# Windowed attention and routed experts on one core: interleaving the two, with block-diagonal attention and a different softmax denominator

## The chip, the cores and the metric

The kernel runs on one core of one Trainium2 chip. The metric is the device time of that core for one whole execution, in microseconds (us). Runs of one kernel are quoted as a median. Each run also has a granted TensorE clock, averaged over its span as a share of full speed. One execution of each kernel was taken with a profile. Profile times are from the start of that execution's span.

In the profile's lines PE is TensorE's matmuls, PEld its weight loads, DVE is VectorE, ACT is ScalarE, POOL is GpSimd. `L128` is line 128 of that kernel's source. Line numbers differ between kernels, so follow the tile names.

## The reference

Sliding-window causal attention over 8 batches, 8 heads, 576 positions and head size 64 (window 64), followed by a mixture of 8 experts with one expert per batch. The expert is chosen from the mean over the positions of that batch's attention output.

```python
scores = scale * np.matmul(q, k.transpose(0, 1, 3, 2))
mask = (rel >= 0) & (rel < 64)                 # rel = query position - key position
attn = softmax(np.where(mask, scores, -1e9))
x = matmul(attn, v) -> [B, 576, 512]

pooled = x.mean(axis=1)                        # [B, 512]
e_idx  = argmax(pooled @ w_gate, axis=1)       # one expert for a whole batch
gate_w = softmax(logits)[e_idx]
out[b] = gate_w[b] * (relu(x[b] @ w1[e]) @ w2[e])   # 512 -> 1024 -> 512
```

One fact of this decides what can overlap: batch b's expert is not known until all of batch b's attention is done, but it does not depend on any other batch.

## The kernel before

The kernel has two stages. The first walks over 32 head pairs (8 batches, 4 pairs). Two heads sit in the two halves of the partitions, so most matmuls are pairs of 64x64 ones:

```python
for bb in range(B):
    for hp in range(NHP):
        # ... loads: q, k, v of both heads, runs of 256 B in HBM ...
        vt = asb.tile(...);  nc.scalar.copy(out=vt, in_=vn)          # cast of v
        for (tl, dst) in ((qn, qT), (kn, kT)):                       # transposes
            for st in range(4):
                nc.tensor.matmul(out=tp[:, ts(st, 128)], lhsT=tl[:, st]..., rhs=ident, ...)
            nc.scalar.copy(out=dst[:, 0:512], in_=tp)
            # ... the last 64 columns in the same way ...
        stage_a2(preva)      # scores of the pair before
        stage_b(prevb)       # values and denominator of the pair before that

def stage_a2(st):
    # 18 matmuls 64x64: sps / tp4 <- kT, qT
    nc.scalar.activation(out=pt[:, 0:8, :], in_=sps, func=AF.Exp, scale=scale)
    nc.scalar.activation(out=pt[:, 8, :], in_=tp4, func=AF.Exp, scale=scale)
    nc.vector.tensor_tensor(out=pt, in0=pt, in1=bandm, op=ALU.mult)  # the band mask

def stage_b(prev):
    # 40 matmuls 64x64: avp <- pt, vt (values);  lbp <- pt, ones64 (denominator)
    nc.scalar.copy(out=avs, in_=avp[:, 0:S])
    nc.scalar.copy(out=lbs, in_=lbp[:, 0:S])
    nc.vector.reciprocal(out=rl, in_=lbs)
    nc.vector.tensor_tensor_reduce(out=xT[:, pbb, php, :], in0=avs, in1=rl, ...
                                   accum_out=pooled[:, php, pbb:pbb + 1])
```

The second stage computes the gates of all 8 batches at once, and then one expert after another:

```python
# ... gates: 4 small matmuls, max, max_index, Exp, reciprocal ...
for bb in range(B):
    # ... loads of w1t and w2t of the chosen expert, cast on the way, 1 MB each in fp16 ...
    for ft in range(8):                            # w1: 64 matmuls, 288 columns each
        # ... php <- w1t, xT ...
        nc.scalar.activation(out=hT[:, ft]..., in_=php[:, :, 0:SC], func=AF.Relu, scale=gwb[:, bb:bb + 1])
    for mt in range(NST):                          # w2: 40 matmuls, 512 columns each
        # ... pso <- hT, w2t ...
        nc.vector.tensor_copy(out=ob[0:n], in_=pso[0:n])
        nc.sync.dma_start(out=out[bb, mt * 128:mt * 128 + n, :], in_=ob[0:n])
```

The softmax here doesn't subtract the row's maximum and nothing guards it: scores larger than these inputs give would overflow.

## Time and profile before

| before | value |
|---|---|
| median of the first 4 runs | 359.99 us (359.88 to 360.04) |
| mean granted clock of the profiled run | 0.776 |
| attention, 9 to 206.7 us | 197.7 us |
| gate and first weights, 206.7 to 217.6 us | 10.9 us |
| experts, 217.6 to 353.6 us | 136.0 us |

The page of the kernel before: the busy time of each engine, then its busy tenths in 40 slices of the span (9 means 90% or more), the granted clock in the same slices, and the DMA packets.

```profile
...
PE 283.4 (79%) x3018; PEld 196.3 (55%) x3018; DVE 190.1 (53%) x179; ACT 185.5 (52%) x356; POOL 130.8 (37%) x189
...
PE   0697878787778786877784216999999999999995
...
DVE  0049997888887978888879920122120303030312
...
PEclk9998565655655656556558556999999999999999
...
DMA packets 141234, 46.91 MB, mean 131 GB/s; under 512 B 124304, under 2 KB 132496, under 8 KB 141200
...
```

PE is 79% busy over the whole span, but its row and the clock row show two different halves. Up to about slice 21 PE is mostly at 7 to 8 tenths and, after a fast start, its clock at 5 to 6; in the last 15 slices both are at 9, but for the end. Busy at a lower clock is not the same work: the first 64 matmuls of w1 took 9.71 us at a mean clock of 0.82, later ones 8.04 us at 1.0. DVE is at 8 tenths in the first half and nearly free in the second.

The same by stage. After the stretch and its length, the columns are: busy us (and instructions) of PE, PEld, DVE, ACT and POOL, the mean granted clock, the DMA share, GB/s.

```profile
...
9.00:206.70 197.70, 146.62 (x2182) 114.31 (x2182) 161.27 (x130) 135.16 (x287) 109.47 (x156) 0.63 1.05 98
206.70:217.60 10.90, 0.80 (x4) 0.60 (x4) 0.97 (x7) 0.56 (x3) 3.28 (x4) 0.50 0.62 104
217.60:353.60 136.00, 135.96 (x832) 81.38 (x832) 26.91 (x39) 47.38 (x64) 9.82 (x12) 0.99 0.94 183
...
```

The middle line is a hole: 0.80 us of PE in 10.9 us. In the third line PE has no gap left: 135.96 us in 136.00. In the first line no engine is full: DVE, the fullest, has 161.27 of 197.70 us, 82%. (The DMA share adds up packets that overlap in time, so 1.05 there does not mean a full DMA.)

Two groups of the kernel before: line, engine, operation, tiles and shapes, count, then busy us and mean ns, then the idle time of the engine just before them.

```profile
...
L128 DVE RECIPROCAL rl<-lbs 128x576 f32<-128x576 f32 x32 | 119.9, 3750 | 25.8 <-ACT lbs L127 25.8
...
L261 DVE COPY ob<-pso 128x512 f32<-128x512 f32 (+1 forms) x40 | 27.6, 690 | 117.2 <-PE pso L257 102.6
...
```

The reciprocal takes 3750 ns for 576 elements per partition, so 119.9 us of the 161 that DVE is busy in attention. A plain copy of 512 elements out of PSUM takes 690 ns.

Its chain of waits, followed back from the last instruction, as shares of the span by engine and by line:

```profile
...
PE 70%; ACT 15%; issue 5%; DVE 4%; DMA 4%; POOL 1%; POOLq 0%; ACTq 0%; DVEq 0%
PE pso L257 20%; PE php L245 18%; PE tp L171 9%; PE lbp L116 8%; ACT pt L101 7%; PE sps L94 6%; PE avp L116 6%; ACT qT L175 5%; DMA w1t<-in_moe_w_dram 2%; DVE rl L128 2%; PE tp L176 2%; ACT kT L175 2%; DMA qn<-in_q_dram 1%; ACT qT L180 1%; 
...
```

### The profile page before, as it was taken

Reading aid. Unit: us, or ns where it says so; the run is one execution under the profiler, and the core shown is the slowest. Engines: PE = TensorE matmul, PEld = TensorE weight load, DVE = VectorE, ACT = ScalarE, POOL = GpSimd, SP = SyncE. Lnnn points to the kernel's source line nnn. Section 1 sums busy time; section 2 is a strip of 40 time slices with the busy share of each in tenths; the row PEclk is TensorE's granted clock in tenths of the full one; section 3 lists DMA queues with packets and bytes.
Section 4 is the critical chain, followed back from the end, with each engine's and each line's share of the span. In section 5 each row is a group of like instructions: output and inputs, shape, how many; then the busy total and the mean of one; then the engine's idle time right before and its main releaser. Section 6 shows DMA issues by size and latency. Waiting matters only on the chain.

```text
span 357.8 us, 7472 instructions
## 1 busy us (share of the span) xinstructions
PE 283.4 (79%) x3018; PEld 196.3 (55%) x3018; DVE 190.1 (53%) x179; ACT 185.5 (52%) x356; POOL 130.8 (37%) x189
## 2 busy tenths in 40 slices
PE   0697878787778786877784216999999999999995
PEld 0475656565656565656563204565647474756562
DVE  0049997888887978888879920122120303030312
ACT  2578777777766767777766102332415160605140
POOL 9969656565656566666500030000000011100000
PEclk9998565655655656556558556999999999999999
DMA  9999999999999999999800049999999999999302
GB/s 125 173 160 142 127 119 94 113 99 116 99 115 94 115 99 114 100 111 100 78 3 2 0 65 198 209 264 180 211 174 222 178 230 179 203 212 156 132 29 105
DMA packets 141234, 46.91 MB, mean 131 GB/s; under 512 B 124304, under 2 KB 132496, under 8 KB 141200
## 3 DMA queue, kind: packets, MB, share of 16 engines
q0 software_dynamic: 96416, 27.26, 77.1%
q1 hardware_dynamic: 44784, 19.18, 21.0%
q8 instruction: 24, 0.39, 0.5%
q14 instruction: 10, 0.08, 0.1%
HBM read 63.95 MB, written 9.44 MB: 205 GB/s over the span
## 4 chain that ended last, share of the span: by engine, by line
PE 70%; ACT 15%; issue 5%; DVE 4%; DMA 4%; POOL 1%; POOLq 0%; ACTq 0%; DVEq 0%
PE pso L257 20%; PE php L245 18%; PE tp L171 9%; PE lbp L116 8%; ACT pt L101 7%; PE sps L94 6%; PE avp L116 6%; ACT qT L175 5%; DMA w1t<-in_moe_w_dram 2%; DVE rl L128 2%; PE tp L176 2%; ACT kT L175 2%; DMA qn<-in_q_dram 1%; ACT qT L180 1%; DVE xT L129 1%
## 5 line engine op out<-in xcount | busy, mean ns | idle before, releaser
L128 DVE RECIPROCAL rl<-lbs 128x576 f32<-128x576 f32 x32 | 119.9, 3750 | 25.8 <-ACT lbs L127 25.8
L249 ACT ACTIVATE hT<-php,gwb 128x576 f16<-128x576 f32 x64 | 47.4, 740 | 90.1 <-PE php L245 90.1
L261 DVE COPY ob<-pso 128x512 f32<-128x512 f32 (+1 forms) x40 | 27.6, 690 | 117.2 <-PE pso L257 102.6
L245 PE MATMUL php<-xT,w1t 128*128 128x288 f16 x512 | 66.4, 290 | 8.3 <-DMA w1t<-in_moe_w_dram 8.3
L116 PE MATMUL avp<-pt,vt 64*64 64x128 f16 (+1 forms) x640 | 70.4, 277 | 2.2 <-DVE pt L103 2.2
L257 PE MATMUL pso<-w2t,hT 128*128 128x512 f16 (+1 forms) x320 | 71.3, 380 | 0.0
L116 PE MATMUL lbp<-pt,ones 64*64 64x128 f16 (+1 forms) x640 | 70.7, 276 | 0.0
L116 PEld LDWEIGHTS <-vt 64*64 64x64 f16 x640 | 54.2, 150 | 25.5 <-issue 22.4
L156 POOL DMA_DIRECT2D qn<-in_q_dram x63 | 55.1, 878 | 25.2 <-PE tp L176 23.0
L245 PEld LDWEIGHTS <-w1t 128*128 128x128 f16 x512 | 49.9, 99 | 25.3 <-issue 11.2
L156 POOL DMA_DIRECT2D kn<-in_k_dram x63 | 54.8, 872 | 18.3 <-PE tp L176 16.7
L116 PEld LDWEIGHTS <-ones 64*64 64x64 f16 x640 | 55.8, 153 | 7.2 <-issue 5.2
L257 PEld LDWEIGHTS <-hT 128*128 128x128 f16 (+1 forms) x320 | 31.4, 100 | 37.2 <-issue 3.4
L238 POOL DMA_DIRECT2D w1t<-in_moe_w_dram x8 | 6.0, 756 | 78.0 <-PE php L245 50.5
L101 ACT ACTIVATE pt<-sps 128x1024 f16<-128x1024 f32 x32 | 33.4, 1044 | 0.4 <-PE tp L94 0.4
L126 ACT COPY avs<-avp 128x576 f32<-128x576 f32 x32 | 20.5, 640 | 22.5 <-PE lbp L116 21.8
L103 DVE TENSOR_TENSOR pt<-pt,bandm 128x1152 f16<-128x1152 f16 x32 | 22.4, 701 | 18.2 <-ACT pt L102 18.2
L94 PEld LDWEIGHTS <-kT 64*64 64x64 bf16 x576 | 26.7, 150 | 9.6 <-issue 9.3
L94 PE MATMUL sps<-qT,kT 64*64 64x128 bf16 x512 | 32.0, 287 | 0.0
L171 PE MATMUL tp<-ident,kn 128*128 128x128 bf16 x128 | 17.1, 281 | 14.0 <-ACT qT L180 13.9
L175 ACT CAST kT<-tp 128x512 bf16<-128x512 f32 x32 | 18.7, 585 | 16.8 <-PE tp L171 16.8
L171 PE MATMUL tp<-ident,qn 128*128 128x128 bf16 x128 | 19.1, 302 | 9.4 <-DMA qn<-in_q_dram 9.4
(49 smaller groups left out, 188.4 us busy)
## 6 DMA issues: line engine op xcount, KB each, us to landing
vn<-in_v_dram SPq DMA_DIRECT2D x64, 144.0 KB, 3.2
w1t<-in_moe_w_dram POOLq DMA_DIRECT2D x8, 1024.0 KB, 10.0
w2t<-in_moe_w_dram POOLq DMA_DIRECT2D x8, 1024.0 KB, 10.7
out_dram<-ob SPq DMA_DIRECT2D x32, 256.0 KB, 6.1
qn<-in_q_dram POOLq DMA_DIRECT2D x63, 80.0 KB, 3.5
kn<-in_k_dram POOLq DMA_DIRECT2D x63, 80.0 KB, 3.1
out_dram<-ob SPq DMA_DIRECT2D x8, 128.0 KB, 6.2
bandm<-bandm SPq DMA_DIRECT2D x1, 256.0 KB, 4.5
```

Source lines behind the costliest of these rows:

```text
L94: nc.tensor.matmul(out=sdst[p0:p0 + 64, :], lhsT=pkT[p0:p0 + 64, ts(j, 64)], rhs=pqT[p0:p0 + 64, j * 64:j * 64 + 128], start=True, stop=Tr ...
L101: nc.scalar.activation(out=pt[:, 0:8, :], in_=sps, func=AF.Exp, scale=scale)
L103: nc.vector.tensor_tensor(out=pt, in0=pt, in1=bandm, op=ALU.mult)
L116: nc.tensor.matmul(out=op[p0:p0 + 64, qlo:qhi], lhsT=lh, rhs=ppt[p0:p0 + 64, j, qlo - 64 * j:qhi - 64 * j], start=st, stop=sp, tile_positi ...
L128: nc.vector.reciprocal(out=rl, in_=lbs)
L156: nc.gpsimd.dma_start(out=tl[:, :, hh, :], in_=tf[hidx:hidx + 640].rearrange("(st p) d -> p st d", p=128))
L171: nc.tensor.matmul(out=tp[:, ts(st, 128)], lhsT=tl[:, st].rearrange("p h d -> p (h d)"), rhs=ident, start=True, stop=True)
L175: nc.scalar.copy(out=dst[:, 0:512], in_=tp)
L245: nc.tensor.matmul(out=php[:, sc, 0:SC], lhsT=w1t[:, kb, ts(ft, 128)], rhs=xT[:, bb, kb, ts(sc, SC)], start=(kb == 0), stop=(kb == 3))
L249: nc.scalar.activation(out=hT[:, ft].rearrange("p (sc s) -> p sc s", sc=2), in_=php[:, :, 0:SC], func=AF.Relu, scale=gwb[:, bb:bb + 1])
L257: nc.tensor.matmul(out=pso[0:n], lhsT=hT[:, fb, mt * 128:mt * 128 + n], rhs=w2t[:, fb, :], start=(fb == 0), stop=(fb == 7))
L261: nc.vector.tensor_copy(out=ob[0:n], in_=pso[0:n])
```

## The change

The intent is to make the second half's tight TensorE work fill the first half's holes, and to make attention cheaper:

1. Work is cut into units (four head pairs of 512 positions and one packed tail of 64 positions x 8 heads per batch: 40 units) and expert chunks (18 per batch). The program order is written by hand: each unit has three slots into which chunks are put, starting `LAG = 10` units after the first unit. Each batch has its own gate.
2. The VectorE reciprocal becomes Ln and then Exp(-x) on ScalarE. Exp and Ln are in one table set, which is loaded once at the start.
3. Pairs of 64x64 matmuls become 128x128 ones with a block-diagonal stationary operand (`kbd`, `vbd`, `onesbd`), whose zero blocks are written once.
4. Each partition takes four successive rows of q and k, so runs in HBM are 1 KB instead of 256 B. v goes straight into `vbd`, cast in the load.
5. The PSUM copies `avs` and `lbs` go: the multiply-reduce reads PSUM.

The diff, cut to its core:

```diff
+TB=1;MB=3;KM='d';RM='adadadada';WM='adad'
+LAG=10
 ...
+        nc.gpsimd.dma_start(out=t[:, lo:hi],
+            in_=src[b, lo:hi, 0:SM].rearrange("h (p r) d -> p h (r d)", r=4))
 ...
+    def unit_t(b, i):            # 16 transposes, to alternating column halves
+                for r in range(4):
+                    for hh in range(2):
+                        p0 = 64 * hh
+                        nc.tensor.transpose(tp[p0:p0 + 64, n, r], t[:, 2 * i + hh, ts(r, 64)], ident)
+            nc.vector.tensor_copy(out=qT, in_=tp[:, 0])
+            # kbd[p0:p0+64, :, p0:p0+64] <- tp[p0:p0+64, 1], strided, one copy for each half
 ...
+    def unit_s(b, i):            # 8 matmuls 128x128, two Exp, two masks
+    def unit_a(b, i):            # 2 + 8 matmuls: lb <- onesbd, pe/po ; av <- vbd, pe/po
-            nc.scalar.copy(out=avs, in_=avp[:, 0:S])
-            nc.scalar.copy(out=lbs, in_=lbp[:, 0:S])
-            nc.vector.reciprocal(out=rl, in_=lbs)
+            nc.scalar.activation(out=ln, in_=lbf, func=AF.Ln)
+            nc.scalar.activation(out=rl, in_=ln, func=AF.Exp, scale=-1.0)
             nc.vector.tensor_tensor_reduce(
-                out=xT[:, pbb, php, :], in0=avs, in1=rl,
+                out=xm[:, i], in0=av.rearrange("q r p -> q (r p)"), in1=rl,
 ...
+    def gate1(b):                # one batch: logits, argmax, then the loads of w1t and w2t
+    def w1_chunk(b, ft):         # 4 matmuls of 512 columns; the ninth: 32 matmuls of 64 columns
+    def w2_chunk(b, r, half):    # 4 matmuls of 512 columns; the last: 16 of 256, two column halves
 ...
+    def moe(slot):
+        t = slot - 3 * LAG
+        want = min(len(todo), (t * NC) // (3 * NU)) if t > 0 else 0
+        while done[0] < want:
+            todo[done[0]]()
+            done[0] += 1
+    with tc.manual_schedule():
+        # ... loads of batches 0, 1 and 2 ...
+        for u in range(n + 3):
+            if u + 1 < n:
+                unit_t(*units[u + 1])
+            moe(3 * u)
+            if u < n:
+                unit_s(*units[u])
+            if u >= 6 and (u - 6) % NU == 0:
+                gate1((u - 6) // NU)
+                # ... then the q, k, v loads of the batch three further on ...
+            moe(3 * u + 1)
+            if 1 <= u <= n:
+                unit_a(*units[u - 1])
+            moe(3 * u + 2)
+        # ... the chunks left over ...
```

## The prediction

> **What bounds the kernel now.** The busy table by stretches shows two stages that do not overlap. Attention runs to 206.7 us; there TensorE is about 80% busy by record, but the granted clock is 0.55 to 0.71, and VectorE is about 84% busy (119.9 us of it in 32 reciprocals of 3750 ns). The chain of waits alternates between small matmuls and ScalarE copies and exponentials: about 6 us per head pair. From 206.7 to 217.6 us TensorE is almost idle: gate, then 7.9 us for the first weights. From 217.6 to 353.6 us the experts run back to back on TensorE at clock 1.0: 8.04 us (w1, 64 matmuls, 126 ns each) plus 8.75 us (w2, 40 of 219 ns) per batch, VectorE and ScalarE mostly idle.
>
> **What the change does.** Attention units (four head pairs and one packed tail per batch) are interleaved with expert chunks, ten units behind. The reciprocal becomes Ln and Exp on ScalarE; the PSUM copies avs and lbs go; 64x64 matmul pairs become block-diagonal full-array ones; q and k come in runs four times as long; v is cast in its load.
>
> **Costs.** Estimates from durations in the trace:
> - TensorE, full clock, per batch: w1 32x219 ns plus 32 short ones of about 60 ns; w2 32x219 ns plus 1 to 1.8 us: 17 us, as before. Attention: a main unit (16 transposes, 8 score matmuls, 10 for values and sums) about 2 us, a tail 1.3 us; 10 us per batch with the gate. 27 us times 8: 217 us.
> - VectorE: a 512-element PSUM copy took 690 ns, the 1152-element mask 701 ns, the multiply-reduce 745 ns. A main unit (qT, two strided k copies, two masks, one reduce) 3.3 us; a batch with tail, relus, output copies and gate 22 us, 176 us in all, against 190.
> - ScalarE: the exponential took 1044 ns for 1024 elements and 320 ns for 128, so 0.63 us for 512. A batch 16.5 us, 133 us in all, plus some 16 us of zeroing at the start.
> - DMA: 82,000 q/k packets of 256 B become 16,000 of 1 KB plus 8,000 small ones. By the Trainium skill ("DMA: Bandwidth & Descriptors", "Why small descriptors are slow") this helps; early in this trace a 256 B packet took about 15 ns of each engine. Estimated need 23 us per batch, under TensorE's 27.
>
> TensorE stays the limit. Timeline: first exponential at 16 us (loads, zeroing); ten attention-only units at 3.8 us, limited by VectorE and a clock that is not full, 38 us; 33 mixed units at 5.15 us of TensorE work, 5.4 with stalls, 178 us; 26 left-over expert chunks, 24 us; drain 3 us. Sum 259; I predict 258 us, range 238 to 284. The critical-path gain is the overlap: attention's waits and the gate gap are filled with expert matmuls.
>
> **What would show it.** TensorE over 85% busy from 55 us on, granted clock above 0.9 there; no idle stretch around a gate; VectorE 165 to 195 us, ScalarE 140 to 160 us; DMA packets about 80,000; a pure expert tail of 24 us.
>
> **What would make it wrong.** The Trainium skill ("TensorE: Matmul & The Clock Gate", "Part 4: PE-mode transpose") says transposes do not count as activity for the clock. If the mix stays cold, expert matmuls double and the result nears 300 us. Strided k copies dearer than 690 ns would make VectorE the limit. PSUM pools with one buffer could couple the engines. The first weights queue behind three batches of loads (10.6 MB, about 35 us), which can delay the first experts by 5 to 10 us. Faster: transposes to the two column halves may overlap.
>
> Chances: faster by over 2% 0.98, within 2% 0.01, slower 0.01.

## The result, and the profile after

| | before | after |
|---|---|---|
| median | 359.88 us (15 runs, 357.3 to 360.26) | 241.52 us (10 runs, 240.71 to 243.61) |
| ratio, 95% interval | 1 | 0.6727 (0.6708 to 0.6745) |
| span and mean clock of the profiled run | 357.8 us, 0.776 | 241.2 us, 0.982 |

A ratio in this document is the mean time of one kernel's fast runs over the mean time of the other's in the same rounds, so it is not quite the ratio of the medians beside it. The change is faster, and 241.5 us lies inside the predicted range of 238 to 284, 16.5 us under the point of 258.

The page of the kernel after, the same parts as shown of the kernel before.

```profile
...
PE 213.9 (89%) x2336; PEld 128.2 (53%) x2336; DVE 158.1 (66%) x444; ACT 130.4 (54%) x237; POOL 89.3 (37%) x128
...
PE   0486668399999999999999999999989999999992
...
DVE  4578977938756895878488866788567854522411
...
PEclk9999997979999999999999999999999999999998
...
DMA packets 81995, 40.77 MB, mean 169 GB/s; under 512 B 48176, under 2 KB 73776, under 8 KB 81968
...
```

PE does less busy time (213.9 us instead of 283.4), and is at 9 tenths from the ninth slice to the last but one, with a single 8; the clock row is 9 except for two slices of 7 and the last. The packets fell from 141,234 to 81,995.

The kernel after by stage, columns as before: attention alone, the mixed stage, and the expert chunks left over.

```profile
...
10.00:48.00 38.00, 25.36 (x356) 18.77 (x356) 30.97 (x85) 23.58 (x43) 28.93 (x42) 0.96 1.54 154
48.00:213.00 165.00, 163.43 (x1805) 96.97 (x1806) 115.53 (x335) 91.44 (x174) 51.77 (x68) 0.99 1.25 182
213.00:237.00 24.00, 23.80 (x162) 11.65 (x158) 6.35 (x10) 6.46 (x10) 0.00 (x0) 1.00 0.67 152
...
```

In the mixed stage PE is busy 163.43 of 165.00 us at clock 0.99. There is no hole around a gate any more. What remains of attention's waiting is in the first 48 us.

Where the first of those lines ends, one instruction of the timeline of the kernel after (start, duration, engine, line, operation, tiles, shapes, count; in brackets the idle time before it and what ended it):

```profile
...
48.60 1.89 PE L335 MATMUL ph<-xm,w1t 128*128 128x512 f16 x4 [3.05 <-DMA w1t<-in_moe_w_dram]
```

Every wait of PE from 60 us on in the kernel after (what waited, on what: us in total, times, longest):

```profile
...
PE ph L335 <- DMA w1t<-in_moe_w_dram: 0.8, 1, 0.8
PE ph L335 <- DVE glog L286: 0.2, 1, 0.2
```

1.0 us of waiting in 177 us. TensorE is the limit of the kernel after from 48.6 us on.

Part of one batch on PE in the kernel after, from the timeline. A duration includes the matmul pipeline's latency, so read the work from the distances between starts:

```profile
...
87.94 1.10 PE L342 MATMUL ph<-xt,w1t 128*128 128x64 f16 x32
88.97 0.41 PE L179 MATMUL tpt<-ident,qkt 128*64 128x128 bf16 x8
89.32 1.04 PE L357 MATMUL po<-w2t,hm 128*128 128x512 f16 x4
90.19 0.39 PE L197 MATMUL se<-qT,kbd 128*128 128x128 bf16 x4
90.41 0.36 PE L197 MATMUL so<-qT,kbd 128*128 128x128 bf16 x4
90.61 0.60 PE L357 MATMUL po<-w2t,hm 128*128 128x512 f16 x2
```

The 32 matmuls of 64 columns run from 87.94 to 88.97: 1.03 us with the pipeline's change-over (0.93 us in the tail of the program, 29 ns each). Eight transposes take 0.35 us to the next start. Eight score matmuls of at most 128 columns, each with its own weights, take 90.19 to 90.61, 0.42 us. The next batch's transposes of this kind start at 114.62 us, so the steady period of a batch is 114.62 - 88.97 = 25.65 us.

The two ScalarE steps that stand in the reciprocal's place (3750 ns for 576 elements before), in the kernel after:

```profile
...
L248 ACT ACTIVATE rl<-ln 128x512 f32<-128x512 f32 x32 | 20.2, 631 | 1.0
...
L247 ACT ACTIVATE ln<-lb 128x512 f32<-128x512 f32 x32 | 18.9, 591 | 12.5 <-PE lb L237 12.1
...
```

Two groups of the kernel after whose copies the prediction had both put at 690 ns:

```profile
...
L171 DVE COPY kbd<-tp 64x512 bf16<-64x512 bf16 x64 | 43.7, 684 | 0.4
...
L167 DVE COPY qT<-tp 128x512 bf16<-128x512 bf16 x32 | 13.4, 417 | 3.4 <-PE tp L165 3.4
...
```

And its chain of waits:

```profile
...
PE 45%; DMA 34%; POOL 10%; DVE 4%; issue 3%; ACT 2%; POOLq 0%
DMA km<-in_k_dram 25%; PE ph L335 15%; PE po L357 15%; DMA w1t<-in_moe_w_dram 9%; POOL vbd L91 4%; PE tp L165 2%; POOL qkt L83 2%; PE po L368 2%; PE ph L342 2%; POOL qm L76 2%; PE av L235 1%; PE se L197 1%; DVE hm L323 1%; PE lb L231 1%; DV
...
```

This chain gives DMA 34%, although PE waited 1.0 us after 60 us. From 117.71 to 179.45 us it follows loads of k and w1t, and it enters them at PE's one wait of 0.8 us, while PE was working nearly all along. Both readings are true: PE's waits say what limits the time, and the chain says that the loads come hardly earlier than they are needed. The experiments show which use the DMA share has.

### The profile page after: what moved, and what is told of

Its sections match the earlier page's. It is cut to its first block, busy times and chain, and to the rows that moved or that the text cites. A ratio compares the mean times of both kernels' runs of the same rounds, so it can differ in the third digit from the quotient of the medians.

```text
span 241.2 us, 5845 instructions
## 1 busy us (share of the span) xinstructions
PE 213.9 (89%) x2336; PEld 128.2 (53%) x2336; DVE 158.1 (66%) x444; ACT 130.4 (54%) x237; POOL 89.3 (37%) x128
## 2 busy tenths in 40 slices
DMA packets 81995, 40.77 MB, mean 169 GB/s; under 512 B 48176, under 2 KB 73776, under 8 KB 81968
## 4 chain that ended last, share of the span: by engine, by line
PE 45%; DMA 34%; POOL 10%; DVE 4%; issue 3%; ACT 2%; POOLq 0%
DMA km<-in_k_dram 25%; PE ph L335 15%; PE po L357 15%; DMA w1t<-in_moe_w_dram 9%; POOL vbd L91 4%; PE tp L165 2%; POOL qkt L83 2%; PE po L368 2%; PE ph L342 2%; POOL qm L76 2%; PE av L235 1%; PE se L197 1%; DVE hm L323 1%; PE lb L231 1%; DVE kbd L171 1%
## 5 line engine op out<-in xcount | busy, mean ns | idle before, releaser
L91 POOL DMA_DIRECT2D vbd<-in_v_dram x64 | 47.4, 771 | 81.9 <-DMA w2t<-in_moe_w_dram 33.3
L335 PE MATMUL ph<-xm,w1t 128*128 128x512 f16 x256 | 64.4, 385 | 4.0 <-DMA w1t<-in_moe_w_dram 3.8
L357 PE MATMUL po<-w2t,hm 128*128 128x512 f16 x256 | 62.3, 380 | 0.0
L171 DVE COPY kbd<-tp 64x512 bf16<-64x512 bf16 x64 | 43.7, 684 | 0.4
L249 DVE CUSTOM_DVE_ANT_0 xm<-av,rl 128x512 f16<-128x512 f32 x32 | 22.1, 691 | 29.1 <-ACT rl L248 28.9
L321 ACT ACTIVATE hm<-ph,gwb 128x512 f16<-128x512 f32 x32 | 21.9, 684 | 31.2 <-PE ph L335 31.1
L335 PEld LDWEIGHTS <-w1t 128*128 128x128 f16 x256 | 22.3, 99 | 26.2 <-DMA w1t<-in_moe_w_dram 4.1
L357 PEld LDWEIGHTS <-hm 128*128 128x128 f16 x256 | 21.9, 98 | 21.8
L323 DVE TENSOR_SCALAR hm<-ph,gwb 128x512 f16<-128x512 f32 x32 | 23.7, 741 | 6.1 <-PE ph L335 6.1
L247 ACT ACTIVATE ln<-lb 128x512 f32<-128x512 f32 x32 | 18.9, 591 | 12.5 <-PE lb L237 12.1
L248 ACT ACTIVATE rl<-ln 128x512 f32<-128x512 f32 x32 | 20.2, 631 | 1.0
L203 DVE TENSOR_TENSOR pe<-pe,mask 128x512 f16<-128x512 f16 x32 | 13.6, 424 | 4.3 <-ACT pe L201 3.6
L235 PEld LDWEIGHTS <-vbd 128*128 128x128 f16 x128 | 10.2, 101 | 9.3 <-issue 3.4
## 6 DMA issues: line engine op xcount, KB each, us to landing
w2t<-in_moe_w_dram POOLq DMA_DIRECT2D x8, 1024.0 KB, 16.5
```

The source lines that it names most:

```text
L91: nc.gpsimd.dma_start(out=vt[64 * hh:64 * hh + 64, pr, :, 64 * hh:64 * hh + 64], in_=v[b, 2 * pr + hh].rearrange("(j c) d -> c j d", c=64))
L171: (nc.vector.tensor_copy if KM == 'd' or (KM=='h' and hh==0) else nc.scalar.copy)(out=kb[p0:p0 + 64, :, p0:p0 + 64].rearrange("q j (p r) - ...
L247: nc.scalar.activation(out=ln, in_=lbf, func=AF.Ln)
L248: nc.scalar.activation(out=rl, in_=ln, func=AF.Exp, scale=-1.0)
L249: nc.vector.tensor_tensor_reduce(out=xm[:, i], in0=av.rearrange("q r p -> q (r p)"), in1=rl, scale=1.0, scalar=0.0, op0=ALU.mult, op1=ALU.add,
L321: nc.scalar.activation(out=o, in_=i, func=AF.Relu, scale=g)
```

## The experiments

There are two questions. The first: where do the 118 us come from? The prediction said that the critical-path gain is the overlap, and read attention before as a chain of small matmuls and ScalarE work. The rival was that the reciprocal, or attention's cheaper form, gives much of it without any overlap. The second question: what is the kernel after 16.5 us better than predicted, and what limits it now? All twelve kernels gave correct results.

### Experts after attention

The kernel after with all expert chunks behind all attention units. It needs room for eight batches of attention output, and the weights of batch 2 and later are loaded in the expert stage.

```diff
-LAG=10
+LAG=1000
-    xpool = ctx.enter_context(tc.tile_pool(name="xpool", bufs=3))
+    xpool = ctx.enter_context(tc.tile_pool(name="xpool", bufs=8))
         # gate1: weights loaded here for b < 2 only; otherwise just before w1_chunk(b, 0)
```

> The changed kernel, but all expert chunks come after all attention units. Theory (the overlap is only a part of the gain; the new attention stage by itself is far cheaper): attention alone is limited by VectorE, about 3.4 us per main unit and 2.5 us per tail unit in the changed kernel's trace, so 8 us of start + 8 x 16 us = 137 us, then the experts at 15.9 us per batch as in the pure tail of the changed kernel = 127 us, then 4 us: 268 us, 262 to 285. Rival (the overlap is nearly the whole gain): attention alone takes about the 207 us of before, total 330 us or more. Clock: if full-array matmuls by themselves release the clock, the attention stage here shows over 0.8 granted; if it was the expert matmuls in the mix, it falls to the 0.55 to 0.7 of before and a unit takes over 4 us.

Measured: 295.27 us, ratio to the kernel before 0.8224 (0.8171 to 0.8276). The stages of this kernel, columns as before:

```profile
...
8.00:160.00 152.00, 105.25 (x1430) 77.45 (x1430) 118.32 (x374) 88.16 (x171) 73.01 (x100) 0.84 1.16 118
...
163.00:291.00 128.00, 127.57 (x893) 63.22 (x890) 38.45 (x56) 36.88 (x56) 9.84 (x12) 0.99 0.86 170
...
```

Attention alone takes 152 us (before: 197.7), and the experts 128 us (before: 136.0). So of the 118 us, about 64 us (359.2 to 295.3) come without any overlap, and 54 us (295.3 to 241.5) are the overlap's, taken in this order: an interleaving of the old attention was not run. With the overlap TensorE's idle time falls from 59.2 to 27.3 us, and its busy time, for the same 2336 matmuls, from 235.8 to 213.9 us at a higher mean clock (0.904 and 0.982 in the profiled runs). The rival's number, over 330, is out too. The theory's own 262 to 285 was missed because attention took 152 us. The longest group of this kernel's waits on PE is a part of it:

```profile
...
PE tp L165 <- DVE kbd L171: 17.0, 20, 1.8
...
```

This wait is a coupling through the one PSUM buffer of the transposes: PE may transpose the next unit only when DVE has copied the last. In the kernel after, expert chunks stand in the queue between. The 152 us are 3.8 us per unit for 40 units, which is just what the prediction had for an attention-only unit; the expectation written for this run had assumed less. No run with a second such buffer was made, so how much of the 152 us it costs is not shown. The clock in this stage is 0.84, over the 0.8 that the expectation had drawn as its line (before: 0.63), but the attention units alone do not keep TensorE at full speed. Which part of their new form raised it was not tested.

### The reciprocal put back

The kernel after, interleaved, with VectorE's reciprocal in place of Ln and Exp.

```diff
-            nc.scalar.activation(out=ln, in_=lbf, func=AF.Ln)
-            nc.scalar.activation(out=rl, in_=ln, func=AF.Exp, scale=-1.0)
+            nc.vector.reciprocal(out=rl, in_=lbf)
```

> The changed kernel with VectorE's reciprocal in place of Ln and Exp on ScalarE. Theory: VectorE's slack of 83 us in the changed kernel is less than the 120 us that 32 x 3.35 us and 8 x 1.7 us add, so VectorE becomes the limit at about 278 us busy, total 282 to 295 us and gaps on TensorE in every unit. Rival: the reciprocal stays hidden behind TensorE, total under 250 us.

Measured: 320.35 us, ratio 0.894. Its page, busy times and costliest group:

```profile
...
PE 235.0 (74%) x2336; PEld 136.3 (43%) x2336; DVE 276.3 (87%) x484; ACT 87.2 (27%) x157; POOL 89.5 (28%) x128
...
L246 DVE RECIPROCAL rl<-lb 128x512 f32<-128x512 f32 x32 | 107.2, 3350 | 0.5
...
```

VectorE becomes the limit, as the theory said: it is busy 57.4 to 57.7 of 60 us in each of three middle stretches. The size was missed (282 to 295 were expected), because VectorE has 276.3 us of work and cannot spread it over the whole span: from 255 to 318 us, where mostly expert work is left, it is busy only 38.4 us. The order of instructions on TensorE is unchanged from the kernel after, so this difference of 79 us belongs to the swap alone.

### The swap alone, in the kernel before

```diff
-            nc.scalar.copy(out=lbs, in_=lbp[:, 0:S])
-            nc.vector.reciprocal(out=rl, in_=lbs)
+            nc.scalar.activation(out=lbs, in_=lbp[:, 0:S], func=AF.Ln)
+            nc.scalar.activation(out=rl, in_=lbs, func=AF.Exp, scale=-1.0)
```

> The kernel before with Ln and Exp on ScalarE in place of the copy of the sums and the reciprocal. Theory (the reciprocal is the busiest group, but the chain of waits runs through ScalarE and TensorE): VectorE loses 120 us of work, ScalarE gains 0.65 us per head pair, the total stays within 3% of 360 us. Rival (VectorE with 84% busy was the limit of attention): attention falls from 6 to about 5 us per head pair, total 325 to 335 us.

Measured: 321.32 us, ratio 0.8969 (0.8906 to 0.9031), 38 us faster than before. The theory, no change within 3%, fell. The rival, 325 to 335, was nearer, and the gain is a little larger still. Attention in this kernel:

```profile
...
9.00:167.00 158.00, 123.28 (x2182) 98.41 (x2182) 48.19 (x96) 147.45 (x319) 109.81 (x156) 0.82 1.38 123
...
```

ScalarE is busy 147.45 of 158 us. Only now is ScalarE this stage's fullest engine; before, it was busy 135.16 of 197.7. The timeline of the kernel before, VectorE's lines of one head pair and the last exponential, shows what the busy share and the chain hid:

```profile
...
97.55 3.75 DVE L128 RECIPROCAL rl<-lbs 128x576 f32<-128x576 f32 x1 [0.62 <-ACT lbs L127]
...
99.46 0.32 ACT L102 ACTIVATE pt<-tp 128x128 f16<-128x128 f32 x1
...
101.22 0.69 DVE L103 TENSOR_TENSOR pt<-pt,bandm 128x1152 f16<-128x1152 f16 x1
...
101.83 0.75 DVE L129 CUSTOM_DVE_ANT_0 xT<-avs,rl 128x576 f16<-128x576 f32 x1
...
103.63 3.75 DVE L128 RECIPROCAL rl<-lbs 128x576 f32<-128x576 f32 x1 [1.04 <-ACT lbs L127]
...
```

And VectorE's timeline with the swap:

```profile
...
97.93 0.76 DVE L104 TENSOR_TENSOR pt<-pt,bandm 128x1152 f16<-128x1152 f16 x1 [1.93 <-ACT pt L103]
100.22 0.76 DVE L130 CUSTOM_DVE_ANT_0 xT<-avs,rl 128x576 f16<-128x576 f32 x1 [1.53 <-ACT rl L129]
...
102.47 0.76 DVE L104 TENSOR_TENSOR pt<-pt,bandm 128x1152 f16<-128x1152 f16 x1 [1.48 <-ACT pt L103]
...
```

Before, the exponentials of the pair had ended at 99.78 us, but the mask (`pt<-pt,bandm`) starts at 101.22, because VectorE's queue has the reciprocal in front of it. The values' matmuls need the mask. The whole repeats every 6.08 us (97.55 to 103.63). With the swap VectorE stands idle before each mask and each reduce, and the mask repeats every 4.54 us here (97.93 to 102.47); the mean of the stage is 158 / 32 = 4.94 us, against 197.7 / 32 = 6.18 before.

A limit on this: the tool chain orders the kernel before by itself, and with the swap it chose another order on TensorE and ScalarE. The clock of the stage also rose, from 0.63 to 0.82: of the 39.7 us that the stage became shorter, 23.3 are busy time of the same 2182 matmuls (146.62 to 123.28) and 16.4 are idle time of TensorE. So the swap's worth in this kernel is measured, 38 us, but how much of it is the mask's freed queue, the other order, and the clock was not separated. It stays open.

The three runs so far in one table:

| | reciprocal on VectorE | Ln and Exp on ScalarE |
|---|---|---|
| kernel before | 359.2 | 321.3 |
| new attention, experts after it | not run | 295.3 |
| new attention, interleaved | 320.4 | 241.5 |

The swap is worth 38 us in the old kernel and 79 in the interleaved one. The parts do not add up; each one's worth depends on what the others have left as the limit.

### Transposes grouped by half

The prediction named one chance to be faster: transposes into the two column halves may overlap. Grouping them by half should then cost time.

```diff
-                for r in range(4):
-                    for hh in range(2):
+                for hh in range(2):
+                    for r in range(4):
```

> The changed kernel with the 16 transposes of a unit ordered four of one column half, then four of the other, instead of alternating. Theory: alternating transposes overlap in the two halves of the array, which is why they took 36 ns each and not the 56 ns assumed; in runs of four of one half they take about 55 ns each, 0.57 us becomes 0.85 to 0.9 us per unit, about 10 us in all: 249 to 253 us. Rival: 36 ns is the pace whatever the half; within 2 us of 241.5.

Measured: 242.77 us, ratio 0.6757 (0.671 to 0.6803). That is within 2 us of the kernel after, so by the line drawn beforehand it is the rival's. 16 transposes took 0.59 us instead of 0.57. The single records in the traces, which the timeline adds up, show more. In the kernel after, the transposes start in pairs, 4 ns apart, and from one pair to the next 56 ns pass (119.855 and 119.858, 119.910 and 119.914, ...). Here they start in pairs too, 13 to 30 ns apart, and again every 56 ns (121.298 and 121.311, 121.354 and 121.367, ...). A full matmul of 128 columns also starts 56 ns after the one before it (90.193, 90.249). So two transposes run at a time in either order, and 36 ns (0.57 us / 16) is not the pace of one. What failed in the theory is that grouping by four would keep the halves apart. The next run asks again, with groups of eight.

### Wide transposes in the tail unit, and the last w2 chunk grouped by half

Two tests in one kernel, read separately from the timeline. Tail: four transposes of 128 columns in place of eight of 64 in alternating halves. Last chunk of w2: 16 matmuls ordered by half, eight and eight, instead of alternating.

```diff
-            for h in range(H):
-                p0 = 64 * (h % 2)
-                nc.tensor.transpose(tp[p0:p0 + 64, h // 2], qkt[:, h], ident)
+            for n in range(NP):
+                nc.tensor.transpose(tp[:, n], qkt[:, 2 * n:2 * n + 2].rearrange("p h d -> p (h d)"), ident)
-            for fb in range(8):
-                for c in range(2):
+            for c in range(2):
+                for fb in range(8):
```

> The changed kernel with two edits that are read apart in the trace. (a) The tail unit's eight 64-column transposes become four of 128 columns. If 36 ns per transpose comes from the two column halves working together, a wide one takes about 55 ns; if it is the pace of any transpose, about 36 ns. (b) The sixteen 256-column matmuls of the last w2 chunk, which alternate between the column halves, are grouped eight and eight. If alternating halves overlap, the chunk goes from 0.99 to 1.7 us or more, about 6 us in all; if not, it stays at 1.0 us. Total 241 to 249 us.

Measured: 243.7 us, ratio 0.68. The wide transposes in the timeline of this kernel:

```profile
...
64.82 0.39 PE L178 MATMUL tpt<-ident,qkt 128*128 128x128 bf16 x4
65.04 0.59 PE L356 MATMUL po<-w2t,hm 128*128 128x512 f16 x2
```

Four in 0.22 us, 55 ns each, as expected if the two halves work together; in the kernel after eight took 0.35 us (88.97 to 89.32), 44 ns each. And the grouped chunk:

```profile
...
238.13 1.53 PE L367 MATMUL po<-w2t,ht 128*64 128x256 f16 x16
```

Its 16 matmuls take 1.46 us (91 ns each) against 0.97 to 0.99 us (61 ns) in alternating order. That lies between the 1.0 and the 1.7 of the expectation, and the single records say why. In alternating order they start in pairs 4 ns apart, with 109 ns from pair to pair. In the grouped order they first start singly, 109 ns apart; 6 ns after the fifth a second series begins beside the first, with the same 109 ns; the last four are single again. All eight chunks of this kernel show it. So matmuls into different column halves do run at the same time, and the alternating order of the change uses it. The Trainium skill ("TensorE: Matmul & The Clock Gate", "Part 3: Packing small matmuls — row/col tiling") says that tiles at different positions of the array run concurrently; the traces agree, 61 ns for a matmul with both halves at work against 109 ns within one. The records do not name the half, but the spacing reads as if a matmul for the other half starts about four places before its turn: the ninth beside the fifth here, the fifth beside the first in the run before. That would be why groups of four cost nothing there. With 0.02 us per unit and 1.46 - 0.98 = 0.5 us per batch, this is a matter of a few us in the whole.

### Short runs again

The kernel after with q and k in runs of 256 B, four loads in place of one.

```diff
-            nc.gpsimd.dma_start(
-                out=t[:, lo:hi],
-                in_=src[b, lo:hi, 0:SM].rearrange("h (p r) d -> p h (r d)", r=4))
+            for r in range(4):
+                nc.gpsimd.dma_start(
+                    out=t[:, lo:hi, ts(r, 64)],
+                    in_=src[b, lo:hi, 0:SM].rearrange("h (p r) d -> p h r d", r=4)[:, :, r])
```

> The changed kernel, but q and k come in runs of 64 elements (256 bytes) as before, four loads in place of one: about 12,000 packets become 49,000 for them. Theory of the prediction (the DMA engines need about 23 of TensorE's 27 us per batch, so the long runs are needed): the need rises to 29 us per batch, TensorE waits for q, k or weights, total 255 us or more. Rival: the DMA has slack once attention is spread over the whole time; total under 246 us, the loss only in the first 50 us.

Measured: 266.11 us, ratio 0.7426 (0.736 to 0.7491): 24.6 us slower than the kernel after, as the theory said. The first experts start at 62.5 us instead of 48.6, and PE's waits show loads in the mixed stage too:

```profile
...
PE ph L336 <- DMA w1t<-in_moe_w_dram: 13.2, 4, 5.8
PE tp L166 <- DMA qm<-in_q_dram: 8.7, 8, 4.3
...
```

The bytes moved are the same; only the runs are shorter. The Trainium skill ("DMA: Bandwidth & Descriptors", "Why small descriptors are slow (HBM only)") gives a fixed overhead for each packet, 27% at 256 B. This run agrees in direction, +24.6 us; it does not isolate that percentage. Of the 24.0 us between the two profiled spans, 14.3 are idle time of TensorE (27.3 to 41.6) and 9.7 are the same 2336 matmuls taking longer (213.9 to 223.6 us) at a lower mean clock, 0.945 instead of 0.982. A caveat is that four loads in place of one also raised GpSimd's busy time from 89.3 to 135.2 us, so the issue of the loads is in the number as well. Either way, the DMA side of the kernel after has little slack, although PE does not wait for it as written.

### A lag of 8 units, and the loads of batch 2 behind the first weights

With TensorE full from 48.6 us on, what is left to gain is the first 48.6 us. The obvious step was an earlier start of the experts: `LAG = 8` alone, and `LAG = 8` with batch 2's loads behind batch 0's weights.

```diff
-LAG=10
+LAG=8
         # second kernel also: load_qk(2, 0, 8), load_v(2, 0, 4), load_tail(2)
         # moved from the start to just after gate1(0)
```

> The changed kernel with the experts eight units behind attention in place of ten, nothing else. Theory: the first expert chunk waits for the first weights, which land at 48.6 us whatever the distance; two attention-only units less are done by then, two units' worth of chunks less are left at the end: within 3 us of 241.5 and a longer wait for w1 (8 to 10 us in place of 3). Rival: the distance itself sets when the experts start: 5 us or more faster.

> As the run with the distance of eight, and batch 2's loads are issued after the first experts' weights instead of before them. Theory (the first 50 us are limited by the order of the loads on the one POOL queue): w1 lands at about 40 us, experts start 6 to 8 us earlier, batch 2's loads land about 54 us and cost some of it back: 233 to 239 us. Rival (attention's VectorE pace sets the start): no change beyond 2 us.

Measured: 266.48 us (0.7447) for the lag alone and 271.16 us (0.7574) with the loads moved. Both theories fell: not 3 us either way, nor a gain, but 25 and 30 us of loss. One line of PE's waits in the kernel with lag 8 (its profile was taken in an execution, slow, 271.46 us):

```profile
...
PE ph L335 <- DMA w1t<-in_moe_w_dram: 27.1, 8, 8.8
...
```

Eight times, once for each batch, the longest at the start. The kernel after has the first (3.05 us) and one later wait of 0.8 us. The profile of the second kernel shows the same:

```profile
...
PE ph L335 <- DMA w1t<-in_moe_w_dram: 21.6, 8, 4.5
...
```

There too the same 2336 matmuls take longer, 223.8 us instead of 213.9, at a mean clock of 0.934, so part of the loss is the clock. From the issue of w1 to its landing a median 9.8 us pass in the kernel after, 10.6 here. A gate stands at unit 5b + 6, and the experts of batch b begin at unit 5b + 8 with this lag: two units, about 10 us, for the gate and the load together. With a lag of 10 it is four units, about 20 us. The weights' wait is what the lag buys off, not only the gate's. And the first experts started at 48.28 us, no earlier than before, because they wait for w1 and not for their place in the order. With the loads moved they did start earlier, at 43.46 us, and the whole was still the slowest of the three: an early start alone is not a gain.

### A lag of 12 units

```diff
-LAG=10
+LAG=12
-    xpool = ctx.enter_context(tc.tile_pool(name="xpool", bufs=3))
+    xpool = ctx.enter_context(tc.tile_pool(name="xpool", bufs=4))
```

> The experts twelve units behind attention in place of ten, with a fourth buffer for the attention output that this needs. At a distance of eight the kernel lost 25 us, all of it where TensorE waits for w1 of each batch. Theory (the distance has to cover the gate and the load of the weights, about 16 us or three to four units, and ten is just enough): no waits for w1 at twelve, but two more attention-only units at the start and two units' worth of chunks (7 chunks, 6 us) more at the end where nothing overlaps: 243 to 250 us. Rival (eight was bad for another reason, and more distance keeps helping): under 238 us.

Measured: 246.07 us, ratio 0.6862 (0.6825 to 0.6899), within the expected 243 to 250. No wait for w1 is left; the first experts start at 52.74 us, 4.1 us later than in the kernel after, and the whole is 4.6 us longer than that kernel (241.45). But the late start is not what costs: until then TensorE does more attention, and it is idle for 20.5 us before the first experts, against 22.0 in the kernel after. The loss is a new wait, which the kernel after does not have:

```profile
...
PE ph L335 <- DVE ob L362: 5.5, 5, 1.1
...
```

Five times, for five batches, the first matmul of w1 waits 1.1 us for a PSUM buffer that VectorE empties late (`ob<-po`, behind its copies for the next attention unit). So the range was met for a reason that was not the theory's. 10 lies between two losses, 25 us on one side and 4.6 on the other, but the second comes from a wait that depends on how chunks and units fall together at 12, and neither a lag of 11 nor a fourth such PSUM buffer was run.

### The start in another order

The first experts wait for w1, so w1 should come sooner: batch 2's v and tail loads behind the first w1. In the first of two kernels the chunks of batch 0 also come three slots sooner; the second keeps the lag. Both have the wide tail transposes.

```diff
         load_qk(2, 0, 8)
-        load_v(2, 0, 4)
-        load_tail(2)
 ...
         nc.gpsimd.dma_start(out=w1t, in_=w1e[esl].squeeze(0))
+        if b == 0:
+            load_v(2, 0, 4)
+            load_tail(2)
```

> Three small edits to the changed kernel: the tail's transposes 128 columns wide (0.13 us per batch less), v and tail loads of batch 2 issued after the first w1 instead of before it, and the first batch's chunks allowed three slots earlier. If the first 49 us are limited by what lies ahead of the first w1 in the POOL queue, w1 lands 4 to 5 us earlier and the total falls to 236 to 239 us; if the loads only move the wait to batch 2, it stays at 240 to 243 us.

> The same as the run before it, without the earlier start of the first batch's chunks: w1 lands as early, but the program does not use it before unit ten; 238 to 241 us.

Measured: 243.63 us (0.6796, 0.6761 to 0.683) and 242.65 us (0.675, 0.6719 to 0.6781). Both are above the expected gains (236 to 239, and 238 to 241), and within 1% of the kernel after (241.45). The experts do start sooner, at 43.15 and 45.51 us. But in the first of these kernels PE's timeline has this:

```profile
...
74.80 1.59 PE L337 MATMUL ph<-xm,w1t 128*128 128x512 f16 x4 [4.12 <-DMA w1t<-in_moe_w_dram]
```

Batch 1's weights are now late by 4.12 us (4.19 in the second kernel): they are needed about 5 us sooner than in the kernel after, where batch 1's experts start at 75.75 us, and they are issued at 63.53 us instead of 61.63, behind the loads that were moved back. The start had also won less than 5.4 us, since less attention was done by then: TensorE's idle time before the first experts fell only from 22.0 to 19.7 us (20.1 in the second). The wait only moved.

### The kernel after, once more

> The changed kernel itself once more, so that the three other runs of this call are compared with it on the same chip: 241 to 243 us.

Measured: 241.45 us, ratio 0.6729 (0.6694 to 0.6763), as the first time. None of the variants beats it; no version better than both kernels was found.

## Why the prediction was right or wrong

What it said of the kernel after held: TensorE is the limit, full from the first experts on. Its point was 16.5 us too high, and its account of where the gain comes from was wrong, as the last points say. Term by term (the terms of the prediction add up to 259, the measured ones to 241.1, the profiled span):

| term of the sum | predicted | measured | where |
|---|---|---|---|
| first exponential | 16 | 12.5 | ScalarE's zeroing took 10 us, not 16 |
| ten attention-only units, up to the first experts | 38 | 36.1 | 48.6 - 12.5, with 3.05 us of waiting for w1 |
| 33 mixed units | 178 | 164.4 | 48.6 to 213.06: 4.98 us each, not 5.4 |
| experts left over | 24 | 23.7 | 213.06 to 236.8, 27 chunks and not 26 |
| drain | 3 | 4.4 | 236.8 to the span's end |

- **Mis-sized: the mixed units (13.6 of the 17.9 us between the two sums).** The step was "33 mixed units at 5.15 us of TensorE work, 5.4 with stalls". About half of it is the 0.25 us of stalls: 33 times 0.25 is 8 us, and PE was idle for 1.0 us in all. The other half is TensorE's work: 163.5 us busy over 33 units is 4.95 each (the last of these units have no attention left; with attention a unit is 25.65 / 5 = 5.13). The step "32 short ones of about 60 ns" was wrong: they took 29 ns, 0.93 us for all 32 instead of 1.9. The step "1 to 1.8 us" for the last chunk of w2 took 0.98, its low end, since the column halves overlap. So a batch's experts took 7.01 + 0.93 + 6.91 + 0.99 = 15.84 us, not 17, with attention and gate at 25.65 - 15.84 = 9.8, as predicted (10). A hint was there: the Trainium skill ("TensorE: Matmul & The Clock Gate", "Back-to-back issue gap") gives N / 2.4 + 2.5 ns for an isolated matmul of N columns at full clock, which is 29.2 for 64, though it warns that small ones take longer in a stream with weight loads; here they did not.
- **Mis-sized: the start.** "First exponential at 16 us (loads, zeroing)" was 12.5. ScalarE's zeroing took 10.2 us, not 16, and the first exponential starts when it ends, at 12.48.
- **The ten attention-only units: close, partly by luck.** The term ends where w1 lands, 10.1 us after its issue at 38.46, and not where ten units at VectorE's pace end. The prediction had the queue before the first weights only among its risks, with 5 to 10 us of delay; PE waited 3.05 us.
- **Right:** "granted clock above 0.9", measured 0.99 in the mixed stage; TensorE over 85% busy there, 99%; no idle stretch around a gate; packets of "about 80,000", measured 81,995; a pure expert tail of 24 us, measured 23.7. VectorE's 158.1 us and ScalarE's 130.4 us came out a little below the stated 165 to 195 and 140 to 160. One cause on VectorE is that `qT` took 417 ns instead of the assumed 690. The Trainium skill ("VectorE: DVE Perf Modes", "Why PSUM operands drop a tier") allows a 16-bit PSUM operand a mode faster than a 32-bit one; the trace agrees for the plain copy (417 ns), while the strided `kbd` copy of as many elements took 684.
- **The fear of a cold clock was not needed.** The prediction cited the Trainium skill on transposes that do not count as activity for the clock. With 16 transposes in every full unit the clock still was 0.99 here, with expert matmuls between them; the same units without experts had 0.84. No run isolates the transposes.
- **Wrong, though the number was right: "The critical-path gain is the overlap".** Without any overlap the new kernel takes 295.3 us. 64 of the 118 us are there before the overlap, and 54 are the overlap's.
- **Wrong: the reading of the kernel before.** "The chain of waits alternates between small matmuls and ScalarE copies and exponentials" was copied correctly from the view, but the expectation of the swap run took it for the limit. Swapping the reciprocal away, which had 2% of that chain, made the kernel before 38 us faster and put more work on ScalarE. The chain puts each step down to what came last, and does not show an instruction that stood behind the reciprocal in the same queue.
- **Right, but with less room than it sounds: the DMA.** "Estimated need 23 us per batch, under TensorE's 27" fits a PE that hardly waits, but it is close. Runs of 256 B cost 24.6 us, two units less of lag 25, and every load moved forward made another one late.

Of the swap, one more thing held. The Trainium skill ("ScalarE: Activation LUTs", "Rules for kernel authors") advises one table set for exp and ln together. In the trace of the kernel after there is one table load, of 1283 ns, in 241 us.

## What to carry to other kernels

A chain's share is not the worth of taking the step away: here a step with 2% of the chain was worth 38 us, and the trace shows other work standing behind it in its queue; swap the step alone to find out. When a dependent load stands between two interleaved stages, the lag has to cover the decision and the load (here a distance of two units, about 10 us, gave 25 us of loss, and four units none). Judge such a change by TensorE's idle time and not by when a stage starts: a later start with a lag of 12 had less idle time before it, and an earlier one with a lag of 8 was slower. In this kernel, with TensorE full, every load moved forward made another one late, so look for bytes, runs and matmul columns to save rather than for an order.

## What the Trainium skill lacked or had wrong

- "TensorE: Matmul & The Clock Gate", "Back-to-back issue gap": it gives a sustained 81 ns for a matmul of 128 columns and 131 ns for one of 512, in a stream of weight loads and matmuls. Here eight score matmuls, each with its own weights and at most 128 columns, took 0.42 us (starts 56 ns apart at 128 columns), and those of 512 columns 216 ns from start to start, 219 with the change-overs. The page's formula for a single one, which it calls too low for small matmuls and too high for large ones, fits these runs better: 29.2 ns for 64 columns (measured 29), 55.8 for 128 (measured 56), 109 for 256 in one column half (measured 109), 216 for 512 (measured 216).
- The same page, "Part 3: Packing small matmuls — row/col tiling": it does not say what the order of issue is worth for two column halves. Alternating, 16 matmuls of 256 columns took 0.98 us; eight and eight, 1.46 us, with eight of the 16 still side by side; for transposes in groups of four the order made no difference that could be told (0.57 and 0.59 us), since they still started in pairs, every 56 ns.
- The same page, Parts 1 and 4: it describes the clock's two states, but gives nothing by which the clock of a mixed stream of small matmuls, transposes and gaps could be sized beforehand. The means here were 0.63 (attention before, PE 74% busy), 0.82 (with the swap, 78%), 0.84 (new attention alone, 69%) and 0.99 (mixed with experts).
- "VectorE: DVE Perf Modes": it says that the reciprocal is iterative, but gives no cost for an element. Here it took 3350 ns for 512 elements and 3750 ns for 576, so 6.25 ns for each further element, against 690 ns for a copy of 512.
- "DMA: Bandwidth & Descriptors": no size for what short runs cost a kernel whose DMA queue also has to deliver weights on time. Here 256 B in place of 1 KB for q and k cost 24.6 us of 241.5, with GpSimd's issue time included.
